# Float32 scores of both heads placed side by side, and weight preparation placed later, in a fused attention and FFN kernel

## The chip, the cores and the metric

The kernel runs on one core of one Trainium2 chip. The metric is the time of one execution in microseconds (us) on the device; less is better. The kernel before has a median of 722.2 us over three runs (721.16 to 723.02).

## What is computed

Attention with 4 batches, 8 heads, 768 positions and head size 64, float32. A query sees the keys at most `window` (128) positions back, and besides the first `n_sink` (4) positions. Its output, laid out as 3072 tokens by 512 features, goes through an FFN with 2048 hidden features and a gate.

```python
scores = scale * np.matmul(q, k.transpose(0, 1, 3, 2))
scores = np.where(is_sink | in_window, scores, -1000000000.0)
a = np.exp(scores - np.max(scores, axis=-1, keepdims=True))
a = a / (np.sum(a, axis=-1, keepdims=True) + 1e-09)
x = np.matmul(a, v)                  # to (3072, 512)
h = x @ w_in                         # (512, 2048)
g = h * np.clip(h + 3.0, 0.0, 6.0) / 6.0
out = g @ w_out                      # (2048, 512)
```

## The kernel before, in words

**Attention.** A unit is 256 query positions of one batch; there are 12 units, the four first units of the batches ahead of the others (L211, L212). A slot (`s`) is one pair of heads of one unit, so four slots make a unit and there are 48. One head of the pair lies on partitions 0 to 63 of the tiles `kr` and `qr`, the other on 64 to 127. The first ten slots are `plain` (L226): their scores are float32 matmuls over 64 partitions (L310), each of which the trace shows as two records, and two query tiles `t` per head make four scores in a slot, one of 128 and one of 256 columns per head. Later slots split K and Q into a high and a low part, move these parts together by DMA and use all 128 partitions (L315).

The steps of a slot, by the letters of the order list: `l` loads K and Q, `v` loads V, `k` and `q` split them (nothing in a plain slot), `c.s.h.t` is one score: a matmul, then on VectorE the masked minimum out of PSUM (L317); with the second tile of a head also the soft part (C_soft): exponentials on ScalarE (L339), sum and reciprocal on VectorE (L341, L342), and the norm (`norm`, L325 on ScalarE or L327 on VectorE by the letters of NORM0 while `s < START`, which is 9, and of NORM after). `d` transposes the probabilities (L365) and copies them out, `s` does the sink columns of later slots, `e` multiplies by V (L432); after the second head E_out makes xh and xl, a high and a low part (xl at L448 in plain slots). The tiles xh{p} and xl{p} have two buffers each.

**FFN.** When the fourth slot of a unit is done, its FFN is put into a queue as 34 steps (ffn_steps): for each of 8 weight slices two steps of ffn1 (12 matmuls of 256 columns each, L473), then, two slices later (one for the first two units), two steps of ffn2 (6 matmuls of 512 columns, L499), and two that write out. `f` in the order list drains one step. A step has the number of weight parts that it needs, and drain (L533) takes it only when that many have been loaded; if the first unit's next step isn't due, the second unit's may go.

**Weights.** There are 16 weight parts, w_in and w_out of a slice in turn. `w` loads the next one (load_part, L141): a DMA into a stage tile `st` of 64-bit words, two ScalarE activations (L159, L163) and two VectorE operations (L165, L167) that make a float32 tile `wt` out of them, a copy that rounds to the high part (L169, recorded at L35 on ScalarE; the letters of WHI give its engine), and a subtraction on VectorE that gives the low part (L170). `st` has three buffers, under the tags sb0, sb1 and K, `wt` has two, under w0 and kt; kt and K are those of the later slots' K too. `w.n` queues the part's work on VectorE and ScalarE behind slot n's last minimum and last exponential.

**Order.** The list FIRST (L554) gives the order of the steps of the first slots; from slot 16 on the loop at L613 goes through ORDER. The order of the list sets the priority; the framework's scheduler arranges each engine's instructions by it and by what is ready in its own estimate. `i.n` is keep_busy: n matmuls of 128 columns whose result nobody reads. There are 54 of them in FIRST and 10 ahead of it (L88), and each is two records of L86.

Of the kernel before, what the change touches and what calls it, by code (L numbers as in the profile page):

```python
# [9 lines left out]
F32 = mybir.dt.float32  # L10
# [4 lines left out]
ALU = mybir.AluOpType  # L15
# [29 lines left out]
def attn_ffn_kernel(ctx: ExitStack, tc: tile.TileContext, qx, kx, vx, vfx, vsx, n_sink, window, w_in, w_out, out):  # L45
    nc = tc.nc
    B, NU, NP = qx.shape[0:3]
    NT, DM = out.shape
    NFP = w_in.shape[0]
    H, D, UT = 2 * NP, 64, 256  # L50
# [78 lines left out]
    WOH = [const.tile([P, 2, DM], F32R, name=f"woh{i}") for i in range(NFP)]  # L129
    WOL = [const.tile([P, 2, DM], F32R, name=f"wol{i}") for i in range(NFP)]  # L130
    wide = mybir.dt.size(w_in.dtype) == 8
    WHI, WLO = "A", "D"

    def weng(which, at):
        return {"D": nc.vector, "P": nc.gpsimd, "A": nc.scalar}[which[at % len(which)]]
# [5 lines left out]
    def load_part(hi, lo, src, rows, at):  # L141

        def like(t):
            return t.rearrange("p (a b) -> p a b", a=rows)

        st = work.tile([P, PW, 2], I32, tag=("sb0", "sb1", "K")[at % 3 if at < LAST else at % 2], name="st", bufs=1)
        if not wide:
            st = like(st.rearrange("p n w -> p (n w)").bitcast(F32)[:, 0:PW])
            nc.sync.dma_start(out=st, in_=src)
            split_parts(nc, hi, lo, st, nc.scalar, nc.vector)  # L150
            return

# [8 lines left out]
        nc.scalar.activation(out=low, in_=low.bitcast(U32), func=AF.Copy, scale=2.0 ** -29 * (1 - 2.0 ** -18),  # L163
                             bias=7.5 * 2.0 ** -18 - 0.5)
        nc.vector.scalar_tensor_tensor(out=low, in0=high, scalar=-2 ** 31, in1=low,  # L165
                                       op0=ALU.bitwise_and, op1=ALU.bitwise_or)
        nc.vector.scalar_tensor_tensor(out=it, in0=it, scalar=3, in1=low,  # L167
                                       op0=ALU.logical_shift_left, op1=ALU.bitwise_or)
        copy_r(nc, weng(WHI, at), hi, like(ft))  # L169
        weng(WLO, at).tensor_tensor(out=lo, in0=like(ft), in1=hi.bitcast(F32), op=ALU.subtract)  # L170

    def load_w_in(i):
        load_part(WIH[i], WIL[i], w_in[i], NP, 2 * i)
# [359 lines left out]
    def drain(n):  # L533

        for _ in range(n):
            live = [q for q in queues if q]
            if not live:
                return
            if live[0] is queues[0] and len(live) > 1:
                order = live[0:2]  # L540
            else:
                order = live[0:1]
            for q in order:
                if q[0][0] <= 2 * NFP - len(w_order):
# [7 lines left out]

    FROM = 16
    FIRST = """  # L554
        l.0 l.1 k.0 q.0 v.0 v.1 c.0.0.0 k.1 c.0.0.1 c.0.1.0 c.0.1.1
        i.16 l.2 d.0.0 d.0.1 s.0 q.1 v.2 c.1.0.0 c.1.0.1 i.2 i.4 c.1.1.0 c.1.1.1
        e.0.0 k.2 l.3 e.0.1 q.2 i.6 d.1.0 s.1 w.0 m d.1.1 v.3 c.2.0.0 c.2.0.1 i.4 e.1.0 c.2.1.0 c.2.1.1
        l.4 i.2 k.3 d.2.0 q.3 v.4 d.2.1 c.3.0.0 e.1.1 l.5 c.3.0.1 s.2 i.2 c.3.1.0 c.3.1.1
        e.2.0 k.4 e.2.1 d.3.0 q.4 w i.12 d.3.1 s.3 v.5 e.3.0 c.4.0.0 w.2 c.4.0.1 k.5 c.4.1.0 c.4.1.1
        e.3.1 f s.4 q.5 l.6 w.2 f d.4.0 f v.6 w.3 c.5.0.0 f c.5.0.1 d.4.1 c.5.1.0 f k.6 f v.7 q.6 e.4.0 c.5.1.1  # L560
        l.7 e.4.1 f d.5.0 f.3 d.5.1 f.2 c.6.0.0 s.5 c.6.0.1 w f.2 c.6.1.0 e.5.0 f w.4 c.6.1.1
        k.7 e.5.1 q.7 l.8 w.5 f.2 d.6.0 f c.7.0.0 f d.6.1 f.3 v.8 f.2 s.6 f.2 c.7.0.1 e.6.0 c.7.1.0 c.7.1.1
        l.9 f.2 w e.6.1 k.8 q.8 i.2 f.2 s.7 w.5 w.7 f d.7.0 d.7.1 c.8.0.0 i.4 f c.8.0.1 c.8.1.0 f c.8.1.1
        f v.9 e.7.0 k.9 l.10 e.7.1 f q.9 w.8 f.2 w.6 f.2 d.8.0 c.9.0.0 f w.8 d.8.1 c.9.0.1 v.10 c.9.1.0 c.9.1.1
        s.8 l.11 e.8.0 k.10 f.2 q.10 f e.8.1 w.7 f s.9 d.9.0 d.9.1 c.10.0.0 f w.8 f.2 v.11 f.2 c.10.0.1 f.2 c.10.1.0 l.12 c.10.1.1
        e.9.0 f k.11 e.9.1 f q.11 d.10.0 s.10 f.4 v.12 f.2 c.11.0.0 c.11.0.1 d.10.1 f c.11.1.0 f.2 e.10.0 e.10.1 c.11.1.1
        d.11.0 f k.12 f.2 d.11.1 q.12 v.13 f l.13 c.12.0.0 f k.13 c.12.0.1 c.12.1.0 c.12.1.1
        f.3 s.11 q.13 e.11.0 f l.14 e.11.1 f.2 d.12.0 d.12.1 v.14 f s.12 c.13.0.0 f c.13.0.1 f c.13.1.0 l.15 k.14 c.13.1.1
        e.12.0 f k.15 e.12.1 q.14 d.13.0 f s.13 f c.14.0.0 f d.13.1 f v.15 f e.13.0 c.14.0.1 f c.14.1.0 f c.14.1.1
        e.13.1 q.15 d.14.0 s.14 f l.16 f.2 d.14.1 f.2  # L570
    """

    def slot_E(s, h):
# [14 lines left out]
    def do(step):  # L588
# [203 lines left out]
```

## Time and profile before

| | before |
|---|---|
| median of 3 runs | 722.2 us (721.16 to 723.02) |
| the profiled execution | 722.0 us |
| its span in the trace | 720.2 us |
| TensorE matmul busy | 706.3 us (98%) |
| VectorE busy | 495.9 us (69%) |
| ScalarE busy | 418.4 us (58%) |
| GpSimd busy | 173.7 us (24%) |
| mean granted TensorE clock | 0.998 |

The span goes from the first to the last instruction of the program; the 1.8 us between it and the execution's time lie around it. In the trace PE is TensorE's matmul, PEld its weight load, DVE is VectorE, ACT is ScalarE, POOL is GpSimd, and SPq is the queue on which SyncE issues DMAs. A group names the line, the engine, the operation, output<-inputs by the program's tile names, and the shapes. Matmuls are pipelined and their ends are modelled, so they overlap in the records, and busy time of TensorE includes its fillers. The chain of waits is followed back from the last instruction: each piece is what released the next one, or the instruction ahead of it on its engine.

### The profile page before, as it was taken

To read this page: it belongs to the slowest core of one execution; us is meant where nothing else is said; L and a number is where in the kernel's file an instruction comes from. 1 tells how busy PE (TensorE), PEld (TensorE's weight loads), DVE (VectorE), ACT (ScalarE), POOL (GpSimd) and SP (SyncE) were. 2 spreads that over 40 slices of the span, in tenths; PEclk is the share of its full clock that TensorE was granted. 3 is DMA by queue.
4 is the path that set the end of the run, shared out by engine and by line. 5 is a ranking of instruction groups with operands and counts; after the bars stand their busy time and mean duration, and the time that the engine had idled before them with its cause. 6 is when DMAs were issued, how large, how long until landed. Compare 5 with 4: busy or idle time off the path is not lost.

```text
span 720.2 us, 14250 instructions
## 1 busy us (share of the span) xinstructions
PE 706.3 (98%) x4800; PEld 639.1 (89%) x4800; DVE 495.9 (69%) x1365; ACT 418.4 (58%) x1091; POOL 173.7 (24%) x336
## 2 busy tenths in 40 slices
PE   8999999999999999999999999999999999999996
PEld 7777788989989988998999998998999999998995
DVE  4899996667777676776777777677776776543331
ACT  6998985646656655656656566655655665411211
POOL 1000000000035334334335334334333434200000
PEclk9999999999999999999999999999999999999999
DMA  8756745334544544554554554553553642000000
GB/s 292 247 191 206 261 128 161 84 97 129 128 126 139 138 115 121 144 141 121 141 128 134 136 125 106 153 128 97 140 149 101 154 119 71 31 1 1 30 1 34
DMA packets 53296, 89.10 MB, mean 124 GB/s; under 512 B 8160, under 2 KB 38112, under 8 KB 51168
## 3 DMA queue, kind: packets, MB, share of 16 engines
q1 hardware_dynamic: 53072, 88.11, 44.0%
q8 instruction: 40, 0.66, 0.4%
q14 instruction: 40, 0.33, 0.2%
q10 hardware_dynamic: 144, 0.00, 0.0%
HBM read 42.47 MB, written 6.29 MB: 68 GB/s over the span
## 4 chain that ended last, share of the span: by engine, by line
PE 88%; DMA 4%; ACT 3%; DVE 2%; SPq 2%; issue 1%; POOL 0%; ACTq 0%; DVEq 0%
PE hps L473 35%; PE o L499 35%; PE av L432 7%; PE sp L315 5%; PE pt L365 3%; DMA K<-kt 3%; PE sp L310 2%; SPq L265 1%; DMA st<-in_w_in_dram 1%; PE idle L86 1%; DMA raw<-in_n_sink_dram 1%; ACT Pt L339 0%; ACT Ph L339 0%; DVE kt L30 0%; DVE wt L167 0%
## 5 line engine op out<-in xcount | busy, mean ns | idle before, releaser
L473 PE MATMUL hps<-xh,wih 128*128 128x256 f32 x768 | 220.0, 286 | 1.3 <-ACT wih L35 1.1
L473 PE MATMUL hps<-xl,wih 128*128 128x256 f32 x768 | 216.2, 281 | 1.3 <-DVE xl L448 1.3
L473 PE MATMUL hps<-xh,wil 128*128 128x256 f32 x768 | 217.1, 283 | 0.0
L499 PE MATMUL o<-woh,gh 128*128 128x512 f32 x384 | 155.0, 404 | 0.0
L499 PE MATMUL o<-wol,gh 128*128 128x512 f32 x384 | 151.6, 395 | 0.0
L499 PE MATMUL o<-woh,g 128*128 128x512 f32 x384 | 151.3, 395 | 0.0
L473 PEld LDWEIGHTS hps<-xh,wih 128*128 128x128 f32 x768 | 144.7, 188 | 3.9 <-ACT wih L35 2.2
L473 PEld LDWEIGHTS hps<-xl,wih 128*128 128x128 f32 x768 | 144.9, 189 | 2.6 <-DVE xl L448 1.5
L473 PEld LDWEIGHTS hps<-xh,wil 128*128 128x128 f32 x768 | 144.7, 188 | 0.1
L486 DVE SCALAR_TENSOR_TENSOR gf<-gf,hps 128x512 f32<-128x512 f32 x96 | 65.8, 686 | 86.7 <-ACT gf L485 86.1
L347 POOL TENSOR_TENSOR Pt<-Pt 128x256 f32<-128x256 f32 x64 | 47.7, 745 | 295.9 <-ACT Pt L339 295.8
L485 ACT ACTIVATE gf<-hps,three 128x512 f32<-128x512 f32 x96 | 65.8, 685 | 84.9 <-PE hps L473 83.9
L339 ACT ACTIVATE Pt<-Pt,nb 128x272 f32<-128x272 f32 (+2 forms) x152 | 76.8, 506 | 63.0 <-DVE nb L317 62.5
L325 ACT ACTIVATE Pt<-Pt,rc 128x144 f32<-128x144 f32 (+2 forms) x152 | 55.8, 414 | 61.6 <-DVE rc L342 37.9
L499 PEld LDWEIGHTS o<-woh,g 128*128 128x128 f32 x384 | 72.2, 188 | 16.8
L499 PEld LDWEIGHTS o<-wol,gh 128*128 128x128 f32 x384 | 72.5, 189 | 10.4 <-DVE wol L170 0.3
L499 PEld LDWEIGHTS o<-woh,gh 128*128 128x128 f32 x384 | 72.4, 189 | 10.4 <-ACT woh L35 0.2
L488 DVE TENSOR_TENSOR g<-gf,gh 128x512 fp32r<-128x512 f32 x96 | 70.7, 736 | 0.8
L317 DVE CUSTOM_DVE_ANT_0 Pt<-sp,m_t 128x272 f32<-128x272 f32 x128 | 54.4, 430 | 17.5 <-PE sp L315 16.0
L315 PE MATMUL sp<-K 128*128 128x272 f32 (+2 forms) x304 | 60.5, 287 | 2.5 <-DMA K<-kt 2.5
L383 POOL TENSOR_SCALAR_AFFINE_SELECT ph<-ph 128x256 fp32r<-128x256 f32 x64 | 31.0, 485 | 118.6 <-ACT ph L35 118.6
L315 PEld LDWEIGHTS sp<-K 128*128 128x128 f32 x304 | 50.5, 188 | 9.5 <-DMA K<-kt 2.3
(93 smaller groups left out, 1089.8 us busy)
## 6 DMA issues: line engine op xcount, KB each, us to landing
K<-kt SPq DMA_DIRECT2D x128, 200.0 KB, 3.5
K<-kt SPq DMA_DIRECT2D x152, 64.0 KB, 2.4
st<-in_w_in_dram SPq DMA_DIRECT2D x8, 1024.0 KB, 5.3
st<-in_w_out_dram SPq DMA_DIRECT2D x8, 1024.0 KB, 5.2
kr<-in_kx_dram SPq DMA_DIRECT2D x32, 200.0 KB, 2.4
qr<-in_qx_dram SPq DMA_DIRECT2D x48, 128.0 KB, 2.3
out_dram<-ost SPq DMA_DIRECT2D x24, 256.0 KB, 2.6
vr<-in_vx_dram SPq DMA_DIRECT2D x32, 192.0 KB, 2.6
```

The costliest lines, as they stand in the source:

```text
L315: nc.tensor.matmul(out=sp[:, 0:w], lhsT=Q[:, h, t * P:(t + 1) * P], rhs=K[:, h, part, k0c:k0c + w], start=(part == 0), stop=(part == 1))
L317: d["min"] = nc.vector.tensor_tensor_reduce(out=cell(s, h, t, 0, w), in0=sp[:, 0:w], in1=m[:, 0:w], scale=-SCALE, scalar=3.0e38, op0=ALU.a ...
L325: nc.scalar.mul(out=blk, in_=blk, mul=c)
L339: d["exp"] = nc.scalar.activation(out=blk, in_=blk, func=AF.Exp, scale=-1.0, bias=nb[:, i:i + 1], accum_out=sm[:, i:i + 1])
L347: nc.gpsimd.tensor_tensor(out=both, in0=both, in1=prior, op=ALU.add)
L383: nc.gpsimd.affine_select(out=prior[i], in_=own[i], pattern=[[0, 2], [-1, P]], base=0, channel_multiplier=1, compare_op=ALU.is_gt, fill=0.0)
L432: nc.tensor.matmul(out=o, lhsT=l, rhs=r, start=(j == 0 and (h == 0 or not plain(s))), stop=(j == len(seq) - 1 and (h == 1 or not plain(s))))
L473: nc.tensor.matmul(out=hp[:, half, :], lhsT=l, rhs=r, start=(j == 0), stop=(j == n - 1))
L485: nc.scalar.activation(out=gf, in_=hp, func=AF.Relu, bias=three, scale=1.0)
L486: nc.vector.scalar_tensor_tensor(out=gf, in0=gf, scalar=6.0, in1=hp, op0=ALU.min, op1=ALU.mult)
L488: eng(GLO, state["n"] * NP).tensor_tensor(out=g, in0=gf, in1=gh.bitcast(F32), op=ALU.subtract)
L499: nc.tensor.matmul(out=acc, lhsT=l[:, f, ts_], rhs=r[i][:, f, :], start=(i == 0 and f == 0 and j == 0), stop=(i == NFP - 1 and f == 1 and ...
```

## The change

The four scores of a slot are issued in the order head 0, head 1 of one tile, then of the other, instead of both tiles of head 0 and then of head 1, and in most slots with fewer steps in between. The subtraction that makes the low half of a weight part is no longer done with the load: it is put into a list, and the new step `z` does the oldest one; drain counts a part as loaded only when its low half has been issued. The first load moves from the beginning of slot 2 to its end, and the last ones reach into slot 11. WHI gives the high copy of parts 0 and 12 to VectorE, NORM0 gives the norm of head 0's second tile (256 columns) to VectorE while `s < 9`. FIRST is a new list, with 72 matmuls of keep_busy instead of 54.

```diff
@@ -129,7 +129,7 @@
     WOH = [const.tile([P, 2, DM], F32R, name=f"woh{i}") for i in range(NFP)]
     WOL = [const.tile([P, 2, DM], F32R, name=f"wol{i}") for i in range(NFP)]
     wide = mybir.dt.size(w_in.dtype) == 8
-    WHI, WLO = "A", "D"
+    WHI, WLO = "DAAAAAAAAAAADAAA", "D"
 
     def weng(which, at):
         return {"D": nc.vector, "P": nc.gpsimd, "A": nc.scalar}[which[at % len(which)]]
@@ -167,7 +167,13 @@
         nc.vector.scalar_tensor_tensor(out=it, in0=it, scalar=3, in1=low,
                                        op0=ALU.logical_shift_left, op1=ALU.bitwise_or)
         copy_r(nc, weng(WHI, at), hi, like(ft))
-        weng(WLO, at).tensor_tensor(out=lo, in0=like(ft), in1=hi.bitcast(F32), op=ALU.subtract)
+        low_parts.append((lo, like(ft), hi))
+
+    low_parts = []
+
+    def low_part():
+        lo, whole, hi = low_parts.pop(0)
+        nc.vector.tensor_tensor(out=lo, in0=whole, in1=hi.bitcast(F32), op=ALU.subtract)
 
     def load_w_in(i):
         load_part(WIH[i], WIL[i], w_in[i], NP, 2 * i)
@@ -318,7 +324,7 @@
                                        scalar=3.0e38, op0=ALU.add, op1=ALU.min,
                                        accum_out=d["nb"][:, i:i + 1])
 
-    NORM0, NORM = "DADA", "AAAA"
+    NORM0, NORM = "DDDA", "AAAA"
 
     def norm(e, blk, c):
         if e == "A":
@@ -541,7 +547,7 @@
             else:
                 order = live[0:1]
             for q in order:
-                if q[0][0] <= 2 * NFP - len(w_order):
+                if q[0][0] <= 2 * NFP - len(w_order) - len(low_parts):
                     q.pop(0)[1]()
                     break
 
@@ -552,22 +558,22 @@
 
     FROM = 16
     FIRST = """
-        l.0 l.1 k.0 q.0 v.0 v.1 c.0.0.0 k.1 c.0.0.1 c.0.1.0 c.0.1.1
-        i.16 l.2 d.0.0 d.0.1 s.0 q.1 v.2 c.1.0.0 c.1.0.1 i.2 i.4 c.1.1.0 c.1.1.1
-        e.0.0 k.2 l.3 e.0.1 q.2 i.6 d.1.0 s.1 w.0 m d.1.1 v.3 c.2.0.0 c.2.0.1 i.4 e.1.0 c.2.1.0 c.2.1.1
-        l.4 i.2 k.3 d.2.0 q.3 v.4 d.2.1 c.3.0.0 e.1.1 l.5 c.3.0.1 s.2 i.2 c.3.1.0 c.3.1.1
-        e.2.0 k.4 e.2.1 d.3.0 q.4 w i.12 d.3.1 s.3 v.5 e.3.0 c.4.0.0 w.2 c.4.0.1 k.5 c.4.1.0 c.4.1.1
-        e.3.1 f s.4 q.5 l.6 w.2 f d.4.0 f v.6 w.3 c.5.0.0 f c.5.0.1 d.4.1 c.5.1.0 f k.6 f v.7 q.6 e.4.0 c.5.1.1
-        l.7 e.4.1 f d.5.0 f.3 d.5.1 f.2 c.6.0.0 s.5 c.6.0.1 w f.2 c.6.1.0 e.5.0 f w.4 c.6.1.1
-        k.7 e.5.1 q.7 l.8 w.5 f.2 d.6.0 f c.7.0.0 f d.6.1 f.3 v.8 f.2 s.6 f.2 c.7.0.1 e.6.0 c.7.1.0 c.7.1.1
-        l.9 f.2 w e.6.1 k.8 q.8 i.2 f.2 s.7 w.5 w.7 f d.7.0 d.7.1 c.8.0.0 i.4 f c.8.0.1 c.8.1.0 f c.8.1.1
-        f v.9 e.7.0 k.9 l.10 e.7.1 f q.9 w.8 f.2 w.6 f.2 d.8.0 c.9.0.0 f w.8 d.8.1 c.9.0.1 v.10 c.9.1.0 c.9.1.1
-        s.8 l.11 e.8.0 k.10 f.2 q.10 f e.8.1 w.7 f s.9 d.9.0 d.9.1 c.10.0.0 f w.8 f.2 v.11 f.2 c.10.0.1 f.2 c.10.1.0 l.12 c.10.1.1
-        e.9.0 f k.11 e.9.1 f q.11 d.10.0 s.10 f.4 v.12 f.2 c.11.0.0 c.11.0.1 d.10.1 f c.11.1.0 f.2 e.10.0 e.10.1 c.11.1.1
-        d.11.0 f k.12 f.2 d.11.1 q.12 v.13 f l.13 c.12.0.0 f k.13 c.12.0.1 c.12.1.0 c.12.1.1
-        f.3 s.11 q.13 e.11.0 f l.14 e.11.1 f.2 d.12.0 d.12.1 v.14 f s.12 c.13.0.0 f c.13.0.1 f c.13.1.0 l.15 k.14 c.13.1.1
-        e.12.0 f k.15 e.12.1 q.14 d.13.0 f s.13 f c.14.0.0 f d.13.1 f v.15 f e.13.0 c.14.0.1 f c.14.1.0 f c.14.1.1
-        e.13.1 q.15 d.14.0 s.14 f l.16 f.2 d.14.1 f.2
+        l.0 l.1 k.0 q.0 k.1 v.0 v.1
+        c.0.0.0 q.1 c.0.1.0 c.0.0.1 c.0.1.1 i.12 l.2 d.0.0 d.0.1 s.0 k.2
+        c.1.0.0 c.1.1.0 c.1.0.1 c.1.1.1 e.0.0 i.4 v.2 i.2 s.1 e.0.1 l.3 d.1.0 d.1.1 q.2 v.3
+        c.2.0.0 c.2.1.0 i.4 c.2.0.1 c.2.1.1 e.1.0 l.4 s.2 e.1.1 i.4 k.3 q.3 m i.12 d.2.0 w.0 v.4 d.2.1
+        c.3.0.0 c.3.1.0 w.1 l.5 c.3.1.1 z c.3.0.1 e.2.0 z i.4 k.4 w.2 i.8 z q.4 i.2 d.3.0 e.2.1 w.3 s.3 d.3.1 i.6 l.6
+        c.4.0.0 z v.5 e.3.0 c.4.1.0 c.4.0.1 k.5 c.4.1.1 i.8 e.3.1 w.2 z f w.2 f i.4 d.4.0 q.5 d.4.1 f s.4 f i.2 z
+        c.5.0.0 c.5.1.0 c.5.0.1 v.6 c.5.1.1 w.4 f.2 e.4.0 f w.4 f e.4.1 v.7 k.6 l.7 z q.6 w.4 f.2 z d.5.0 d.5.1
+        c.6.0.0 c.6.0.1 s.5 z c.6.1.0 c.6.1.1 f.2 e.5.0 e.5.1 k.7 q.7 w f w l.8 f z z d.6.0 s.6 k.8 f.4
+        c.7.0.0 v.8 c.7.1.0 d.6.1 c.7.0.1 q.8 c.7.1.1 e.6.0 e.6.1 f l.9 f.2 w f z
+        c.8.0.0 d.7.0 f.2 d.7.1 f c.8.0.1 f.3 v.9 f.3 c.8.1.0 c.8.1.1 f.5 s.7 k.9 f e.7.0 e.7.1 f q.9 l.10 f.2 d.8.0 d.8.1 v.10 w.7 s.8
+        c.9.0.0 c.9.1.0 z e.8.0 f c.9.0.1 f l.11 c.9.1.1 s.9 f e.8.1 f k.10 f q.10 d.9.0 f d.9.1 w.8
+        c.10.0.0 f v.11 k.11 f c.10.0.1 f q.11 f c.10.1.0 z e.9.0 e.9.1 w.9 c.10.1.1 l.12 f s.10 z d.10.0 f.2 d.10.1 f v.12
+        c.11.0.0 f c.11.1.0 c.11.1.1 f c.11.0.1 f e.10.0 k.12 w.10 s.11 l.13 f.2 e.10.1 q.12 d.11.0 k.13 f d.11.1 f
+        c.12.0.0 f c.12.1.0 c.12.0.1 c.12.1.1 e.11.0 f.3 e.11.1 z f.2 v.13 d.12.0 l.14 d.12.1 f q.13 f
+        c.13.0.0 c.13.1.0 s.12 c.13.1.1 c.13.0.1 k.14 f.3 v.14 q.14 e.12.0 s.13 e.12.1 f l.15 v.15 f d.13.0
+        c.14.0.0 c.14.1.0 c.14.0.1 d.13.1 c.14.1.1 f e.13.0 k.15 f l.16 f.3 d.14.0 s.14 d.14.1 e.13.1 q.15 f
     """
 
     def slot_E(s, h):
@@ -592,6 +598,8 @@
             drain(n[0] if n else 1)
         elif kind == "w":
             weights(n[0] if n else None)
+        elif kind == "z":
+            low_part()
         elif kind == "i":
             keep_busy(n[0])
         elif kind == "m":
```

## Rows read from the trace of the kernel before

**Rows 1.** Busy time of each engine by stretch; after PEclk the DMA share, GB/s

```profile
core 0: us, PE busy (x) PEld busy (x) DVE busy (x) ACT busy (x) POOL busy (x), PEclk, DMA share, GB/s
6.70:35.00 28.30, 27.11 (x185) 22.35 (x184) 21.54 (x76) 26.16 (x65) 0.63 (x3) 1.00 0.82 300
35.00:60.00 25.00, 23.59 (x144) 19.48 (x143) 24.10 (x54) 23.23 (x46) 0.00 (x0) 1.00 0.62 216
60.00:90.00 30.00, 28.85 (x180) 24.14 (x179) 27.44 (x62) 26.36 (x49) 0.00 (x0) 1.00 0.67 222
90.00:110.00 20.00, 19.98 (x134) 17.43 (x133) 19.09 (x37) 17.37 (x33) 0.00 (x0) 1.00 0.46 134
...
600.00:700.00 100.00, 100.00 (x666) 91.19 (x665) 42.16 (x99) 24.38 (x55) 9.24 (x20) 1.00 0.08 22
```

**Rows 2.** Chain of waits in order of time, 0 to 130 us: start, us, what

```profile
10.24 1.02 issue
...
12.13 0.59 ACT st L163
...
14.41 0.76 ACT wt L159
...
22.25 1.12 DVE wt L167
...
35.33 1.14 DVE st L165
...
36.61 1.12 DVE wt L167
...
38.25 1.93 PE hps L473 x14
...
50.59 1.43 PE hps L473 x12
...
70.43 0.98 ACT Ph L339 x4
...
72.73 1.07 ACT wih L35
...
78.72 0.69 ACT gf L485
79.41 0.95 ACT wih L35
```

**Rows 3.** Timeline of ScalarE: start, us, then the instruction; idle before it in brackets

```profile
10.21 1.14 ACT L159 ACTIVATE wt<-st 128x1024 f32<-128x1024 f32 x1 [0.91 <-DMA st<-in_w_in_dram]
```

**Rows 4.** Timeline of TensorE, neighbours of one line merged

```profile
5.84 0.93 PE L310 MATMUL sp<-kr,qr 64*128 64x128 f32 x8 [0.53 <-DMA qr<-in_qx_dram]
6.71 3.84 PE L86 MATMUL idle<-rel 128*128 128x128 f32 x32
...
18.02 0.92 PE L310 MATMUL sp<-kr,qr 64*128 64x128 f32 x4
...
56.80 0.92 PE L310 MATMUL sp<-kr,qr 64*128 64x128 f32 x6
```

**Rows 5.** Busy time by stretch of L310 alone: PE, PEld, clock, DMA

```profile
10.00:32.50 22.50, 5.52 (x24) 3.11 (x24) 1.00 0.78 275
32.50:100.00 67.50, 10.79 (x48) 5.63 (x48) 1.00 0.59 200
```

**Rows 6.** ScalarE groups, 35.1 to 110.1 us: count, busy us, mean ns, idle before

```profile
L35 ACT ACTIVATE wih<-wt 128x1024 fp32r<-128x1024 f32 x6 | 6.3, 1058 | 0.0
...
L325 ACT ACTIVATE Ph<-Ph,rc 128x256 f32<-128x256 f32 x12 | 5.9, 501 | 0.0
```

**Rows 7.** VectorE groups of the same stretch

```profile
L317 DVE CUSTOM_DVE_ANT_0 Ph<-sp,m 128x256 f32<-128x256 f32 x11 | 4.6, 417 | 0.8 <-PE sp L310 0.8
L41 DVE CAST gh<-gf 128x512 fp32r<-128x512 f32 x8 | 3.4, 420 | 0.0
L317 DVE CUSTOM_DVE_ANT_0 Ph<-sp,m 128x128 f32<-128x128 f32 x10 | 2.9, 285 | 0.4 <-PE sp L310 0.4
L327 DVE TENSOR_SCALAR Ph<-Ph,rc 128x128 f32<-128x128 f32 x10 | 2.7, 279 | 0.0
```

## Prediction

> **What bounds the kernel now.** I read the stretches first, then the chain of waits in order of time, then single groups. In the stretches [rows 1] the reader is to see two halves. From 600 us on TensorE is busy 100.00 of 100 us while VectorE needs 42.16 and ScalarE 24.38: nothing but matmul is left, so whatever time TensorE wastes earlier is still missing at the end, and whatever it saves earlier comes off the end. Until 110 us all three engines are close to full: ScalarE 26.16 of 28.30 us before 35, VectorE 24.10 of 25, 27.44 of 30 and 19.09 of 20 after that. The change acts there; the loop from slot 16 on is not touched.
>
> A busy TensorE is not a useful one, since fillers count as busy, so the chain decides [rows 2]. Up to 38.25 us it is mixed: pieces on ScalarE and VectorE that belong to weight parts (L159, L163, L165, L167) stand between attention steps. At 10.24 the norm of slot 0's second head waits 1.02 us because ScalarE first does weight part 0's L159, for which it sat idle 0.91 us until the transfer landed [rows 3]. The five pieces 12.13, 14.41, 22.25, 35.33 and 36.61 add 0.59 + 0.76 + 1.12 + 1.14 + 1.12 = 4.73 us, so 5.75 us of the chain up to the first unbroken run of FFN matmuls are weight work. From 38.25 to 110 the chain is nearly all TensorE; the two breaks of over a microsecond are those that end with the weight copies at 72.73 and 79.41 (3.4 us from 70.43, 1.6 us from 78.72). So a TensorE instruction saved there counts, as long as VectorE, with 0.90 + 2.56 + 0.91 = 4.4 us free in 75, follows.
>
> **The change, part by part.**
>
> *Scores side by side.* In slot 0 of the kernel before, nothing stands between the four scores on TensorE, and the eight records (float32 makes two of each matmul) take 0.93 us; from slot 1 on the two heads are apart and one head alone takes 0.92 [rows 4]. At 56.80 six records of both heads take 0.92 too. So the two heads, on partitions 0 to 63 and 64 to 127, already run at the same time when they are neighbours, at no cost to either. By stretches [rows 5] slots 1 to 3 take 5.52 us and slots 4 to 9 take 10.79. At 0.93 a slot that would be 2.79 and 5.58: 2.7 us saved before the FFN, 5.2 us in it. The first 2.7 us I cost at nothing: fillers stand in the same stretch (16 in the 3.84 us after slot 0), so TensorE waits there. Of the 5.2, the new order keeps slots 4 to 7 together but for single steps; in slot 8 transposes and FFN steps stand between all the pairs, and in slot 9 between the second ones. I leave these two out, a third of six slots, and take 3.4. Ends: 0 (the engine that reads the scores sets the pace) and 5.2.
>
> *Weights later.* w.0 moves from slot 2's beginning to its end, behind d.2.0, and the loads come in ones and twos until slot 11 (before: slot 10). Each load still issues one transfer on SyncE, two activations and a copy on ScalarE and three operations on VectorE. The transfer moves later with it, past v.3 and l.4 on SyncE's queue, which gives these two their turn earlier, and ScalarE no longer sits waiting for it at 10 us. Parts 0 to 3 still come ahead of the first FFN step, so their work cannot leave the stretch, only move out of attention's way. ScalarE is the fullest there. It loses one 256-wide norm in each of four slots and part 0's copy [rows 6]: with 0.50 and 1.06 us, and about 0.1 of each covered by its neighbour, 4 x 0.4 + 1.0 = 2.6 us. I take 2.6 us off the start of the FFN. Ends: 0 (the weights are merely missed later) and 5.75 (all of it leaves the chain).
>
> *Norms and two copies on VectorE.* The 256-wide norm there is bounded by the 128-wide one, 0.28, and by twice that; the reading of a 256-wide score, 0.42, is nearest [rows 7], 0.34 behind a neighbour. Part 0's and part 12's copy, 1024 wide, lie between one and three times the 512-wide cast at 0.42; I take 0.75, as twice the columns with one start. Slots 4 to 8 and part 12 fall into the stretch where VectorE is 91 to 96% busy: 5 x 0.34 + 0.75 = 2.5 us. Slots 0 to 3 and part 0, 2.1 us, fall where it has 6.8 us free [rows 1] and cost nothing; without that cover they would be 2.1 more. Of the 2.5 I count 1.5, since the chain there runs on TensorE and 4.4 us are free. Ends: 0 and 4.6 for both stretches.
>
> *Low halves as steps.* The same subtraction, 16 times as before, placed by hand. The buffer that it reads stays taken until then, so the second load after it (and k.11, which shares one with part 13) waits for it; behind k.11 on ScalarE queue slot 11's activations and its scores. By then unit 1's FFN steps are there to run; cost nothing, at most one subtraction where they are not.
>
> *Fillers.* There are 54 matmuls of keep_busy before and 72 after, all 18 new ones ahead of the FFN. At 3.84/16 = 0.24 us [rows 4] they are 4.3 us of TensorE, which the 2.7 us of scores saved there and TensorE's waiting, which the fillers of before already fill, cover; where TensorE is what holds the start up, +1.6.
>
> *New order.* Counted through the lists, 22 FFN steps are issued ahead of slot 8's scores where it was 14, but 63 by the end of the list where it was 71. A step is 12 small matmuls, 1.43 us [rows 2], so about 11 us of FFN move behind the list and none disappears. They end in the last stretch, where TensorE is full anyway: cost nothing. Attention that runs further ahead has to wait for the two xh buffers; what it waits for is FFN, so TensorE is not idle.
>
> **Sum.** -2.6 (start) - 3.4 (scores) + 1.5 (VectorE) = -4.5 us on the profiled execution's 722.0, which is 0.2 below the median of the runs. That gives 717.5.
>
> **Rivals.**
>
> *VectorE reads the scores no faster.* A slot's four scores cost it 2 x (0.29 + 0.42) = 1.4 us [rows 7] by durations, over the 0.93 that TensorE then needs. If each pair waits for that, the 3.4 us turn into waits: -2.6 + 1.5, 720.9. Against it: between two slots TensorE has FFN steps, so the pace of one slot need not show. The Trainium skill, TensorEngine Tiling (Array Packing), Performance Considerations, says the same as a rule: tiling speeds up the matmul engine but not the emptying of PSUM, which may become the bottleneck. By that rule the scores would bring nothing, and the trace agrees so far as 1.4 exceeds 0.93. Chance 0.2, most of it within the band of no change.
>
> *VectorE becomes the bound (slower).* The place is 35 to 110 us. If neither its 6.8 free us before 35 nor its 4.4 after are used, every added operation shows, 2.1 + 2.5 = 4.6 us, and neither start nor scores help, since TensorE then waits for g and for low halves: 722.0 + 4.6 = 726.6; with the 2.1 still covered, 724.5. It decides from the point where added work exceeds free time in the FFN's stretch: 2.5 against 4.4 speaks against it, 95% busy for it. Chance 0.15.
>
> *The start falls away.* All 5.75 us leave the chain, the breaks at 70 and 78 us go (5.0) because unit 1 is there earlier, and scores bring 3.4: with half of the breaks, 722.0 - 5.75 - 2.5 - 3.4 + 1.5 = 711.9. For it: the chain shows exactly those pieces. Against it: the weights have to be made sometime, on engines that are full. Chance 0.2.
>
> *The order doesn't do what it says.* The trace shows instructions on ScalarE in another order than the list has them (part 0's first activation ahead of slot 0's last norm, though w.0 stands after slot 1 there), so the placing need not survive, and slots 4 and 6 were partly together already. Then -1 to -2: 720.5. It shares the chance of the first rival.
>
> **How the numbers follow.** Forecast 0.45, about 715 to 719.8; quick start 0.2; no gain 0.2; VectorE 0.15. About 0.3%, 2.2 us, is what a measurement of this kernel can tell from no change. So faster 0.65, same 0.2, slower 0.15. The range goes from 711, just past the quick start, to 724.5, which leaves out the worst of the VectorE case: some 2 in 10 stay outside. The forecast's own range is 715 to 720.
>
> **What would show it.** Scores: L310 in slots 4 to 7 as groups of eight records of about 0.93, and under 8 us of L310 from 32 to 100 us. Start: no wait of a norm behind L159 at 10 us, and the unbroken run of FFN matmuls from 35 to 36 us (38.25 before). VectorE: over 97% busy from 35 to 110 if the slower rival is right, with hps and o waiting for g, wil or wol. The last weight part is done later than before, without a wait of o. The prediction is wrong if the FFN starts no earlier, or if TensorE's gaps in 38 to 110 grow by what L310 loses.

## The result and the profile after

The changed kernel takes 715.32 us (median of 4 runs, 715.13 to 716.19) against 722.28 us of the kernel before on the same chip (4 runs, 721.16 to 723.02). The ratio is 0.9907, with a 95% interval from 0.989 to 0.9924: 7.0 us, or 0.9%, faster. The forecast was 717.5 us in a range from 711 to 724.5; the sign was right, the gain 2.5 us too small, and the time stands at the low end of the forecast's own 715 to 720. A second sample of the changed kernel, shown below, gave 0.9913. One execution of the run with the pairs alone took 1144.77 us at a mean clock of 0.556, and no ratio uses it.

In the changed kernel the lines after the edit stand six further down: the scores' L310 is L316, the norms' L325 and L327 are L331 and L333, the FFN's L473 and L499 are L479 and L505, and the subtraction for the low half is L176. The profiled execution took 716.19 us, the slowest of the four.

The head of the profile page: span, then busy time of each engine.

```profile
span 714.5 us, 14315 instructions
...
PE 703.5 (98%) x4836; PEld 640.3 (90%) x4836; DVE 496.0 (69%) x1376; ACT 413.3 (58%) x1080; POOL 173.2 (24%) x336
```

The same stretches as in [rows 1], with the loop from 200 to 600 us added:

```profile
core 0: us, PE busy (x) PEld busy (x) DVE busy (x) ACT busy (x) POOL busy (x), PEclk, DMA share, GB/s
6.70:35.00 28.30, 27.66 (x209) 23.51 (x207) 24.98 (x83) 26.05 (x60) 0.74 (x4) 1.00 0.81 304
35.00:60.00 25.00, 23.48 (x173) 21.25 (x173) 23.63 (x49) 21.77 (x41) 0.00 (x0) 1.00 0.71 253
60.00:90.00 30.00, 30.00 (x200) 25.89 (x200) 29.32 (x75) 26.10 (x55) 0.00 (x0) 1.00 0.53 169
90.00:110.00 20.00, 20.00 (x129) 17.79 (x130) 18.05 (x47) 15.96 (x39) 0.00 (x0) 1.00 0.58 187
...
200.00:600.00 400.00, 399.24 (x2802) 367.35 (x2802) 292.56 (x849) 242.24 (x689) 156.25 (x293) 1.00 0.48 126
600.00:700.00 100.00, 100.00 (x654) 90.97 (x653) 36.59 (x67) 17.38 (x31) 3.68 (x8) 1.00 0.03 11
```

Three things are to be seen. Before 35 us VectorE took over work (24.98 us where it was 21.54), yet ScalarE is as busy as before, 26.05 against 26.16: what it was relieved of was filled up again, by weight parts (the two activations of a part, L159 and L163, take 11.5 us there where they took 9.2). From 35 to 110 us ScalarE needs 63.8 us where it needed 67.0, and VectorE, with 71.0 of 75 us, is no fuller than before (70.6). And TensorE has no gap from 60 to 90 us, where it had 1.15 us.

The scores' line alone, the counterpart of [rows 5] (busy time of TensorE, then of its weight loads, clock, DMA):

```profile
10.00:32.50 22.50, 3.86 (x25) 2.06 (x26) 1.00 0.79 287
32.50:100.00 67.50, 6.94 (x48) 3.77 (x48) 1.00 0.63 213
```

48 records that took 10.79 us take 6.94. The timeline of TensorE (start, duration, instruction, idle time before it in brackets) has the start of the FFN and a pair of heads in one group. First the FFN's first matmul in the kernel before, then the changed kernel:

```profile
35.13 0.37 PE L473 MATMUL hps<-xh,wih 128*128 128x256 f32 x1
```

```profile
36.95 0.36 PE L479 MATMUL hps<-xh,wih 128*128 128x256 f32 x1
...
38.22 0.83 PE L86 MATMUL idle<-rel 128*128 128x128 f32 x6
38.81 0.37 PE L479 MATMUL hps<-xl,wih 128*128 128x256 f32 x1
...
44.81 0.93 PE L316 MATMUL sp<-kr,qr 64*128 64x128 f32 x8
47.26 0.47 PE L505 MATMUL o<-woh,gh 128*128 128x512 f32 x1 [1.52 <-DVE gh L41]
```

Eight records of both heads take 0.93 us at 44.81, what one head alone took at 18.02 in [rows 4]. The first FFN matmul comes at 36.95 us, 1.8 us later than before, and the run without fillers between its matmuls starts at 38.81, against 38.25 in [rows 2]. So the FFN does not start earlier. (Second traces of the two kernels, from the last experiment below, have 35.26 and 36.95.)

Of the profiled spans' 5.7 us (720.2 to 714.5), busy sums explain part: TensorE's gaps between 6.7 and 700 us shrink from 6.3 to 3.7 us (2.6 us), the scores after 10 us from 16.3 to 10.8 (5.5 us), and fillers after 6.7 us grow from 14.16 to 18.01 (-3.85 us). That is 4.3 us; the other 1.4 such sums cannot place, since neighbouring matmuls overlap in them.

### The profile page after: what moved, and what is told of

Its sections match the earlier page's. It is cut to its first block, busy times and chain, and to the rows that moved or that the text cites. A ratio compares the mean times of both kernels' runs of the same rounds, so it can differ in the third digit from the quotient of the medians.

```text
span 714.5 us, 14315 instructions
## 1 busy us (share of the span) xinstructions
PE 703.5 (98%) x4836; PEld 640.3 (90%) x4836; DVE 496.0 (69%) x1376; ACT 413.3 (58%) x1080; POOL 173.2 (24%) x336
## 5 line engine op out<-in xcount | busy, mean ns | idle before, releaser
L479 PE MATMUL hps<-xh,wih 128*128 128x256 f32 x768 | 219.2, 286 | 0.3 <-DVE tmp L460 0.3
L479 PE MATMUL hps<-xh,wil 128*128 128x256 f32 x768 | 216.6, 282 | 0.0
L479 PE MATMUL hps<-xl,wih 128*128 128x256 f32 x768 | 215.9, 281 | 0.0
L505 PE MATMUL o<-woh,gh 128*128 128x512 f32 x384 | 154.2, 402 | 1.5 <-DVE gh L41 1.5
L505 PE MATMUL o<-woh,g 128*128 128x512 f32 x384 | 151.4, 395 | 0.0
L505 PE MATMUL o<-wol,gh 128*128 128x512 f32 x384 | 151.3, 394 | 0.0
L479 PEld LDWEIGHTS hps<-xh,wih 128*128 128x128 f32 x768 | 144.6, 188 | 2.0 <-PE sp L321 0.5
L479 PEld LDWEIGHTS hps<-xl,wih 128*128 128x128 f32 x768 | 144.8, 188 | 1.2
L479 PEld LDWEIGHTS hps<-xh,wil 128*128 128x128 f32 x768 | 144.6, 188 | 0.1
L331 ACT ACTIVATE Pt<-Pt,rc 128x144 f32<-128x144 f32 (+2 forms) x152 | 55.3, 414 | 60.4 <-DVE rc L348 36.4
L505 PEld LDWEIGHTS o<-woh,g 128*128 128x128 f32 x384 | 72.2, 188 | 17.3 <-issue 0.3
L505 PEld LDWEIGHTS o<-woh,gh 128*128 128x128 f32 x384 | 72.3, 188 | 11.8 <-ACT gf L491 1.9
L505 PEld LDWEIGHTS o<-wol,gh 128*128 128x128 f32 x384 | 72.4, 189 | 10.3
```

The lines of the kernel that those rows point to most:

```text
L331: nc.scalar.mul(out=blk, in_=blk, mul=c)
L479: nc.tensor.matmul(out=hp[:, half, :], lhsT=l, rhs=r, start=(j == 0), stop=(j == n - 1))
L505: nc.tensor.matmul(out=acc, lhsT=l[:, f, ts_], rhs=r[i][:, f, :], start=(i == 0 and f == 0 and j == 0), stop=(i == NFP - 1 and f == 1 and ...
```

## The experiments

Each ratio is to the kernel before on the same chip, from 5 to 12 executions; 0.0014 of it is 1 us. The theory after the result: paired scores shorten TensorE's path, and the rest comes from fewer waits in the new order. The rival: the scores were covered anyway, and the work moved between ScalarE and VectorE made the gain.

**Pairs alone.** In the order of before, the four scores of each of slots 0 to 9 are put together where the first stood; nothing else is changed.

```diff
-        i.16 l.2 d.0.0 d.0.1 s.0 q.1 v.2 c.1.0.0 c.1.0.1 i.2 i.4 c.1.1.0 c.1.1.1
+        i.16 l.2 d.0.0 d.0.1 s.0 q.1 v.2 c.1.0.0 c.1.1.0 c.1.0.1 c.1.1.1 i.2 i.4
...
-        k.7 e.5.1 q.7 l.8 w.5 f.2 d.6.0 f c.7.0.0 f d.6.1 f.3 v.8 f.2 s.6 f.2 c.7.0.1 e.6.0 c.7.1.0 c.7.1.1
+        k.7 e.5.1 q.7 l.8 w.5 f.2 d.6.0 f c.7.0.0 c.7.1.0 c.7.0.1 c.7.1.1 f d.6.1 f.3 v.8 f.2 s.6 f.2 e.6.0
```

> The kernel before with one edit in its order list: the four scores of each plain slot stand together at the place of the first. Theory (paired scores are TensorE time saved in the FFN's stretch): the busy time of L310 in slots 4 to 9 falls from 10.79 to about 6 us and the time falls by 3 to 4 us, to about 718.5. Rival (the pairing shows only in the order that the weights have in the changed kernel, since VectorE reads the scores no faster): L310 falls as much and the time stays within 1.5 us of 722.3.

Measured: 721.16 us, ratio 0.9988 (0.9975 to 1.0002). That looks like the rival, but the stretches (columns as above) say otherwise:

```profile
20.00:25.00 5.00, 2.57 (x16) 2.08 (x14) 4.83 (x14) 5.00 (x13) 0.00 (x0) 0.89 0.77 243
25.00:30.00 5.00, 5.00 (x18) 3.16 (x18) 3.63 (x11) 4.02 (x11) 0.00 (x0) 0.50 0.51 200
30.00:35.00 5.00, 3.44 (x23) 2.92 (x22) 3.34 (x10) 4.01 (x9) 0.00 (x0) 0.93 0.92 289
```

and TensorE's timeline just there:

```profile
24.02 0.66 PE L365 MATMUL pt<-ident_r,Ph 128*128 128x128 f32 x2 [2.43 <-DVE Ph L327]
...
27.29 1.23 PE L310 MATMUL sp<-kr,qr 64*128 64x256 f32 x4
```

With the scores shorter, TensorE was done early and waited 2.43 us for a norm; the granted clock fell to 0.50, the 1.2 GHz level, and came back to 1.00 only between 30 and 35 us. Read from the three means, it was low for 1.1 + 5.0 + 0.7 = 6.8 us. The kernel before holds 1.00 in that stretch [rows 1]. Its compared executions list a mean clock of 0.990 to 0.996 over the span, those of the kernel before beside them 0.997 to 1.0. The Trainium skill, TensorE: Matmul & The Clock Gate, section on HAM oscillation, says that waits between groups of matmuls can put the engine back to the slow clock; this trace agrees (a wait of 2.43 us, then 0.50).

**Pairs and sixteen fillers.** The same with fillers put where TensorE waits.

```diff
-        l.4 i.2 k.3 d.2.0 q.3 v.4 d.2.1 c.3.0.0 c.3.1.0 c.3.0.1 c.3.1.1 e.1.1 l.5 s.2 i.2
-        e.2.0 k.4 e.2.1 d.3.0 q.4 w i.12 d.3.1 s.3 v.5 e.3.0 c.4.0.0 c.4.1.0 c.4.0.1 c.4.1.1 w.2 k.5
+        l.4 i.2 k.3 i.10 d.2.0 q.3 v.4 d.2.1 c.3.0.0 c.3.1.0 c.3.0.1 c.3.1.1 e.1.1 l.5 s.2 i.2
+        e.2.0 k.4 e.2.1 i.6 d.3.0 q.4 w i.12 d.3.1 s.3 v.5 e.3.0 c.4.0.0 c.4.1.0 c.4.0.1 c.4.1.1 w.2 k.5
```

> The paired scores in the order of the kernel before (as in e1_pairs_alone), with 16 more matmuls of keep_busy where TensorE waited there, ahead of d.2.0 and d.3.0. Theory (in e1_pairs_alone the pairing's gain was given back because the granted clock fell to 0.5 for 6.8 us after a wait of 2.4 us that score matmuls used to fill): the clock stays at 1.00 from 7 us on and the time falls by 2 to 4 us against e1_pairs_alone's ratio of 0.9988, to about 718.5. Rival (the score time saved was not on the path in that order): the clock stays up and the time stays within 1.5 us of 721.

Measured: 717.07 us, ratio 0.9946 (0.9933 to 0.996): 3.9 us faster than before and 3.0 us faster than the pairs alone. The first stretch, then the scores' line:

```profile
6.70:35.00 28.30, 26.42 (x206) 22.93 (x204) 22.48 (x71) 27.04 (x63) 0.73 (x4) 1.00 0.85 305
```

```profile
32.50:105.00 72.50, 6.25 (x48) 3.43 (x48) 1.00 0.62 209
```

The clock holds 1.00, and the scores, 10.79 us before in this stretch too, take 6.25: 4.5 us of TensorE less, for a gain of 3.9 in the old order, on the old engines and with low halves made at once. The two numbers can't simply be set against each other, though, as the loop of the profiled execution (716.13 us, the fastest of its six) shows:

```profile
200.00:600.00 400.00, 400.00 (x2819) 368.86 (x2818) 296.04 (x853) 245.56 (x696) 160.38 (x296) 1.00 0.50 129
```

TensorE has no gap there. In the kernel before it has 2.5 and 2.0 us in two traces (shown further down), so 2.0 to 2.5 us of this execution's gain lie in a part that no edit touches. From 35 to 110 us, on the other hand, its gaps are 3.5 us where they were 2.6, and the first FFN matmul comes at 36.66 us, 1.5 later than before. How much of the 3.9 us reaches the time through the shorter scores alone is therefore not shown, and the sixteen fillers were not tried without the pairs.

**The change without eighteen fillers.** They are taken out of slot 3's row.

```diff
-        c.3.0.0 c.3.1.0 w.1 l.5 c.3.1.1 z c.3.0.1 e.2.0 z i.4 k.4 w.2 i.8 z q.4 i.2 d.3.0 e.2.1 w.3 s.3 d.3.1 i.6 l.6
+        c.3.0.0 c.3.1.0 w.1 l.5 c.3.1.1 z c.3.0.1 e.2.0 z k.4 w.2 z q.4 i.2 d.3.0 e.2.1 w.3 s.3 d.3.1 l.6
```

> The changed kernel without 18 of its matmuls of keep_busy (those of slot 3's row: 4, 8 and 6), so with 54 as before. Theory (the new fillers hold the clock up while TensorE waits): a stretch at 0.5 appears between 20 and 45 us and the time rises by 1.5 to 4 us above 715.3. Rival (they are TensorE time on the way to the first FFN step): the clock stays at 1.00, the first FFN matmul comes 1 to 4 us earlier than at 36.95 and the time falls by 1 to 4 us.

Measured: 722.02 us, ratio 1.001 (0.9996 to 1.0023): the whole gain is gone. Stretches, and the largest wait of TensorE in the first 130 us (us in total, times, longest):

```profile
25.00:30.00 5.00, 2.10 (x14) 1.73 (x12) 5.00 (x17) 4.90 (x12) 0.00 (x0) 0.92 0.74 283
30.00:35.00 5.00, 4.51 (x17) 3.59 (x18) 4.22 (x8) 4.71 (x8) 0.00 (x0) 0.50 0.61 211
35.00:40.00 5.00, 5.00 (x26) 4.30 (x22) 3.63 (x11) 2.45 (x9) 0.00 (x0) 0.56 0.39 100
```

```profile
PE pt L371 <- DVE Ph L333: 4.3, 2, 3.4
```

With a wait of 3.4 us the clock falls, and it is low for 0.8 + 5.0 + 4.4 = 10.2 us, into the FFN. So matmuls that compute nothing are worth 7 us here, more than the theory's 1.5 to 4. At half speed 10.2 us are at most 5.1 us of work, so the clock can be the larger part of it but not all: TensorE also has gaps of 0.9 us from 60 to 90 us, where the changed kernel has none, and of 1.9 in the loop, where it has 0.8. Why these came is not shown.

**Heads apart again.** In the changed kernel the second head's scores of slots 1 to 9 are set at least one TensorE step behind the first's.

```diff
-        c.5.0.0 c.5.1.0 c.5.0.1 v.6 c.5.1.1 w.4 f.2 e.4.0 f w.4 f e.4.1 v.7 k.6 l.7 z q.6 w.4 f.2 z d.5.0 d.5.1
+        c.5.0.0 c.5.0.1 v.6 w.4 f.2 c.5.1.0 c.5.1.1 e.4.0 f w.4 f e.4.1 v.7 k.6 l.7 z q.6 w.4 f.2 z d.5.0 d.5.1
...
-        c.7.0.0 v.8 c.7.1.0 d.6.1 c.7.0.1 q.8 c.7.1.1 e.6.0 e.6.1 f l.9 f.2 w f z
+        c.7.0.0 c.7.0.1 v.8 d.6.1 c.7.1.0 c.7.1.1 q.8 e.6.0 e.6.1 f l.9 f.2 w f z
```

> The changed kernel with the two heads' scores of slots 1 to 9 set apart by one other TensorE step. Theory (pairing is worth its TensorE time): L316 in slots 4 to 9 rises from 6.94 to about 10.5 us and the time rises by 3 to 4 us above the changed kernel's 715.3, to about 719. Rival (the gain is that of the weights' order and of the backlog): within 1.5 us of 715.3.

Measured: 724.14 us, ratio 1.003 (1.0017 to 1.0043), 9 us slower than the change, more than the theory's 3 to 4. The scores' line:

```profile
32.50:105.00 72.50, 11.03 (x48) 6.21 (x48) 1.00 0.60 202
```

It takes 11.03 us again, 4.1 more than in the changed kernel. The loss is more than that: in the profiled execution (722.72 us, at a mean clock of 0.998) the line also takes 5.52 us from 10 to 32.5 us (3.86 in the changed kernel), TensorE waits 2.5 us for VectorE's norms in the first 130 us (0.4 there), and the first FFN matmul comes at 41.10 us (36.95 there). The slowest executions (725.1 to 727.0) list a mean clock of 0.993 to 0.995. The order was made for scores that come together.

**Low halves made at once.** In the changed kernel the subtraction goes back behind the load, and the steps z fall out.

```diff
         copy_r(nc, weng(WHI, at), hi, like(ft))
-        low_parts.append((lo, like(ft), hi))
+        weng(WLO, at).tensor_tensor(out=lo, in0=like(ft), in1=hi.bitcast(F32), op=ALU.subtract)
...
-        c.4.0.0 z v.5 e.3.0 c.4.1.0 c.4.0.1 k.5 c.4.1.1 i.8 e.3.1 w.2 z f w.2 f i.4 d.4.0 q.5 d.4.1 f s.4 f i.2 z
+        c.4.0.0 v.5 e.3.0 c.4.1.0 c.4.0.1 k.5 c.4.1.1 i.8 e.3.1 w.2 f w.2 f i.4 d.4.0 q.5 d.4.1 f s.4 f i.2
```

> The changed kernel with each low half made with its load, as in the kernel before, and z doing nothing. Theory (low halves as steps of their own cost and bring nothing, since the scheduler places them by priority anyway): within 1.5 us of 715.3. Rival (a low half ahead of scores on VectorE's queue delays attention in the first slots): 2 to 4 us above it, with VectorE's reads of scores waiting behind L170.

Measured: 719.23 us, ratio 0.9954 (0.9941 to 0.9967): 3.4 us slower than the change by the ratios. TensorE's largest waits in the first 130 us:

```profile
PE o L505 <- ACT st L163: 2.1, 1, 2.1
PE pt L371 <- ACT Ph L331: 1.7, 1, 1.7
```

In the changed kernel TensorE waits 1.5 us for gh at the first L505 instead, and 0.3 us for L331. The clock falls to its low level behind each of them, as the stretches from 6.7 to 35 us (mean 0.94) and from 35 to 60 us (0.93) list, but that profile is of the slowest execution (722.82 us, mean clock 0.992 over the span). The two at 0.998 and above took 718.30 and 718.29, so some 3 us are lost without the clock.

**The old engines.** Norms and copies go back to the engines of before.

```diff
-    WHI, WLO = "DAAAAAAAAAAADAAA", "D"
+    WHI, WLO = "A", "D"
...
-    NORM0, NORM = "DDDA", "AAAA"
+    NORM0, NORM = "DADA", "AAAA"
```

> The changed kernel with the norms of head 0's second tile and the copies of weight parts 0 and 12 back on ScalarE. Theory (ScalarE is the fuller engine up to the first FFN step, VectorE after it): the first FFN matmul comes 1 to 2.6 us later than at 36.95, VectorE has 4 us less in 0 to 110, and the time is about 1 us above 715.3. Rival (VectorE is the bound in the FFN's stretch): 1.5 to 4 us below 715.3.

Measured: 717.51 us, ratio 0.9927 (0.9914 to 0.994), 1.0 to 1.4 us slower than the two samples of the change, whose intervals it overlaps. What the theory asked for is in the trace: the first FFN matmul comes 1.0 us later, and VectorE is busy 94.07 us up to 110 us where it is 97.53 in the changed kernel.

```profile
37.93 0.36 PE L479 MATMUL hps<-xh,wih 128*128 128x256 f32 x1
```

So VectorE's new work does no harm, and in this order ScalarE's relief is worth about 1 us at the start of the FFN.

**The new engines in the old order.** The same two constants of the change, put into the kernel with pairs and sixteen fillers.

```diff
-    WHI, WLO = "A", "D"
+    WHI, WLO = "DAAAAAAAAAAADAAA", "D"
...
-    NORM0, NORM = "DADA", "AAAA"
+    NORM0, NORM = "DDDA", "AAAA"
```

> The order of the kernel before with paired scores and 16 more fillers (as in e5_pairs_fillers, ratio 0.9946), and the changed kernel's norms and weight copies on VectorE. Theory (ScalarE is the fuller engine ahead of the FFN, as e4_engines showed in the new order with 0.9927 against 0.9907): 1 to 2 us below e5_pairs_fillers, a ratio near 0.9925. Rival (the moves pay only with the new order's placing of weights): within 0.7 us of 0.9946, or above it.

Measured: 718.18 us, ratio 0.9947 (0.9934 to 0.996), against 0.9946 without them: nothing. In this order the FFN starts no sooner for it (37.60 us against 36.66).

**Late low halves in the old order.** The changed kernel's code with the order of the last run, and each z put six places behind its w.

```diff
-        e.3.1 f s.4 q.5 l.6 w.2 f d.4.0 f v.6 w.3 c.5.0.0 c.5.1.0 c.5.0.1 c.5.1.1 f d.4.1 f k.6 f v.7 q.6 e.4.0
+        e.3.1 f s.4 q.5 l.6 z w.2 f d.4.0 f v.6 w.3 c.5.0.0 z c.5.1.0 c.5.0.1 c.5.1.1 f d.4.1 z f k.6 f v.7 q.6 e.4.0
```

> The code of the changed kernel with the order of e5_pairs_fillers, and each low half as a step six places behind its load. Theory (pairs with fillers, engine moves and late low halves are the whole gain, and the rest of the new order is worth nothing): a ratio of 0.990 to 0.992, like the changed kernel. Rival (the new order as a whole is needed to use late low halves): no better than e11_pairs_engines.

Measured: 724.9 us, ratio 1.0045 (1.0029 to 1.0061), slower than the kernel before. A stretch, and TensorE's largest waits until 130 us:

```profile
90.00:110.00 20.00, 16.92 (x120) 15.37 (x118) 18.89 (x33) 16.07 (x32) 0.00 (x0) 1.00 0.48 140
```

```profile
PE pt L371 <- DVE Ph L333: 2.0, 4, 1.2
PE sp L321 <- DMA K<-kt: 1.9, 1, 1.9
PE o L505 <- ACT gf L491: 1.2, 1, 1.2
```

Only the low halves differ from the run before, and with them when drain lets a step go, since a part counts only with its low half. They cost 7 us (1.0045 less 0.9947). Some of that is clock: three of the six executions list 0.993 or 0.994 and took 725.9 to 726.6 us, while the two at 0.998 took 722.2 and 723.0, 4 to 5 us more than the run before. In the new order it was 3 us dearer to make them at once. So neither place is good in itself; six places was one choice among many, and others weren't tried.

**The first load early.** In the changed kernel w.0 goes back to the beginning of slot 2.

```diff
-        c.2.0.0 c.2.1.0 i.4 c.2.0.1 c.2.1.1 e.1.0 l.4 s.2 e.1.1 i.4 k.3 q.3 m i.12 d.2.0 w.0 v.4 d.2.1
+        w.0 c.2.0.0 c.2.1.0 i.4 c.2.0.1 c.2.1.1 e.1.0 l.4 s.2 e.1.1 i.4 k.3 q.3 m i.12 d.2.0 v.4 d.2.1
```

> The changed kernel with the first weight load back at the beginning of slot 2, all else unchanged. Theory (the scheduler fits part 0 into ScalarE's gaps either way; its place in the list moves little): within 1.5 us of 715.3. Rival (part 0 in the way of slots 0 to 2 is what the kernel before paid at 10 us): 2 to 4 us above it.

Measured: 715.42 us, ratio 0.9916 (0.9902 to 0.9929), the same as the change. ScalarE's timeline shows why, first in the changed kernel and then in this one:

```profile
10.30 1.13 ACT L159 ACTIVATE wt<-st 128x1024 f32<-128x1024 f32 x1 [0.90 <-DMA st<-in_w_in_dram]
11.34 0.49 ACT L331 ACTIVATE Ph<-Ph,rc 128x256 f32<-128x256 f32 x1
```

```profile
10.33 1.14 ACT L159 ACTIVATE wt<-st 128x1024 f32<-128x1024 f32 x1 [1.11 <-DMA st<-in_w_in_dram]
11.37 0.50 ACT L331 ACTIVATE Ph<-Ph,rc 128x256 f32<-128x256 f32 x1
```

Either way ScalarE turns to part 0 at 10.3 us and sits idle for its transfer, as in [rows 3], and the norm stands behind it. Moving w.0 in the list did not move this work in the instruction stream.

**The change without six late fillers.** Those among the first FFN steps are taken out.

```diff
-        c.4.0.0 z v.5 e.3.0 c.4.1.0 c.4.0.1 k.5 c.4.1.1 i.8 e.3.1 w.2 z f w.2 f i.4 d.4.0 q.5 d.4.1 f s.4 f i.2 z
+        c.4.0.0 z v.5 e.3.0 c.4.1.0 c.4.0.1 k.5 c.4.1.1 i.8 e.3.1 w.2 z f w.2 f d.4.0 q.5 d.4.1 f s.4 f z
```

> The changed kernel without the six matmuls of keep_busy that stand among the first FFN steps. Theory (TensorE has work there, so they are on its path): about 1 us below 715.3, since six of them are 12 records at about 0.11 us. Rival (they fill waits): within 0.7 us of 715.3, with idle time in their place.

Measured: 718.83 us, ratio 0.9964 (0.9952 to 0.9976), 4 us slower than the change, with the clock at 1.00 in every stretch. Both theories missed this. Its largest wait in the first 130 us:

```profile
PE o L505 <- DVE gh L41: 2.1, 1, 2.1
```

It was 1.5 us in the changed kernel's first trace and 2.1 us in its second, shown next, so it does not explain the loss by itself. TensorE's gaps from 35 to 110 us are 3.0 us where they were 1.5 (2.1 in the second trace), and instructions far behind the six stand in another order. How much of the 4 us is that order and how much the wait stays open.

**Both kernels once more.** No edit: one more execution of the kernel before and five more of the changed one, to see what repeats.

> The kernel before once more, for a second trace. Theory (part of the gain is in the loop from slot 16 on: TensorE was busy 397.48 of 400 us there before, 399.24 after): again about 397.5 between 200 and 600 us. Rival (that difference is one of single executions): between 398.5 and 400.

> The changed kernel once more, on the same chip as the experiments beside it. Every theory: a ratio of 0.990 to 0.992, granted clock 1.00 from 7 us to the tail, and TensorE busy about 399 of 400 us between 200 and 600 us.

Measured: 721.67 us for the kernel before. The changed kernel took 715.9 us, ratio 0.9913 (0.99 to 0.9926). The loop, first in the two executions of the kernel before and then in the changed kernel's second one:

```profile
200.00:600.00 400.00, 397.48 (x2788) 365.62 (x2788) 295.06 (x843) 243.79 (x690) 159.94 (x299) 1.00 0.50 128
```

```profile
200.00:600.00 400.00, 398.04 (x2791) 366.08 (x2790) 294.88 (x844) 243.86 (x690) 161.94 (x299) 1.00 0.49 128
```

```profile
35.00:60.00 25.00, 22.89 (x156) 20.52 (x155) 22.52 (x48) 19.72 (x38) 0.00 (x0) 0.93 0.67 232
...
200.00:600.00 400.00, 399.21 (x2809) 367.70 (x2808) 293.47 (x851) 242.21 (x690) 157.51 (x296) 1.00 0.48 126
```

TensorE waits 1.2 to 1.8 us less in the loop after the change, although no line there is edited. (The second trace before, 398.04, lies between what the theory and the rival asked for.) The runs shown above have between none (pairs with fillers) and 1.9 us (without eighteen fillers), so what is done ahead of the loop moves its waits. They are mostly for K, before and after:

```profile
PE sp L315 <- DMA K<-kt: 2.5, 5, 1.0
```

```profile
PE sp L321 <- DMA K<-kt: 0.5, 2, 0.3
```

Why its transfers come in better time was not tried and stays open. The profiled execution of the changed kernel lost the clock once, with 0.93 in 35 to 60 us, about 3.5 us at the low level, after a wait for gh of 2.1 us that was 1.5 in the first profile; it took 717.46 us, the slowest of its five. So the fillers do not hold the clock every time.

No variant was faster than the changed kernel.

## Why the prediction was right, and where its terms were wrong

**Scores side by side: right about TensorE, its share of the time not shown.** The term was -3.4 us. The line loses 3.85 us in the stretch that the prediction named, 6.94 us is under the 8 us asked for, and the loss did not turn into waits: TensorE's gaps from 38 to 110 us are 1.5 us where they were 1.4. That TensorE's neighbours on different halves of the partitions run at the same time was read correctly from [rows 4]. Where the pairs stand was forecast less well: groups of eight records were to come in slots 4 to 7 and came in slots 5 and 6 alone (44.81 and 57.80 us), while slots 8 and 9, left out of the term, are partly paired too. In time, the pairs with fillers bring 3.9 us, but in the profiled execution 2.0 to 2.5 of its gain lie in the loop. The part before the FFN, costed at nothing, cannot be parted from this.

**VectorE reads no faster: the rival fell.** Reading four scores still takes VectorE 1.4 us in the changed kernel, longer than the 0.93 us of TensorE, but the time did not stay at the rival's 720.9. By the rule of the Trainium skill, TensorEngine Tiling (Array Packing), Performance Considerations, which speaks of a fourfold speedup, the emptying of PSUM may become the limit; no run here shows it.

**Start of the FFN: wrong.** The step that failed is "I take 2.6 us off the start of the FFN", and the prediction's own sign, wrong "if the FFN starts no earlier", came true: the first FFN matmul comes 1.8 us later, and the unbroken run begins at 38.81 us where 35 to 36 was forecast. Two things were missed. ScalarE's freed time went in part to the next weight part: before 35 us its norms fell from 4.1 to 2.0 us, the weight activations rose by 2.3, and it is as busy as before. With the old engines the new order starts at 37.93 us, so the relief is worth 1.0 of the 2.6 us. And something else in the change moves the start back: pairs with fillers alone, in the old order, already start at 36.66 us. What it is there that delays the start was not tried. Part of the reasoning also rested on w.0 leaving attention's way, and it did not: the norm at 10 us waits behind L159 as before. That is what the rival "The order doesn't do what it says" had foreseen, though not with its time, 720.5.

The gain came later and in another form. The fourth low half begins at 35.4 us where it began at 41.1, the ninth at 63.7 where it was 73.8, TensorE has no gap from 60 to 90 us, and by 110 us it has issued 240 of the first and 96 of the second FFN matmuls where it had 230 and 84. That the earlier weights closed the gap is likely but not shown: without six late fillers the ninth low half begins at 63.6 us too, and 0.9 us of gap stay. Of the quick start's price, the 5.75 us off the chain did not come; of the 5.0 us of breaks at 70 and 78 us no more was to be had than the 1.15 us for which TensorE had stood still there.

**Low halves cost nothing: wrong.** "Cost nothing, at most one subtraction" holds for the instruction and not for its place. In the new order the place is worth about 3 us; in the old one late low halves cost 7, or 4 to 5 in the executions that keep the clock. The prediction named the buffer behind them as the price but never asked what VectorE could do first.

**Norms and copies on VectorE: right in sum with ScalarE's relief.** The prices read from the rows held: a norm takes 0.345 us on VectorE and a copy 0.69, together 2.4 us in the FFN's stretch (2.5 forecast). Of these +1.5 us was taken as cost, apart from the 2.6 us of relief, whereas only the sum of both can be measured: -2.6 + 1.5 = -1.1, and undoing the move makes the new order 1.0 to 1.4 us slower. As far as the start tells (1.0 us), the relief was put too high and the cost too high by about as much, which is luck. VectorE stays at 71.0 of 75 us, so the slower rival lacked its condition, work above free time.

**Fillers: the right number for a wrong reason.** Nothing was counted for them because TensorE waits there. True, but they are not idle ballast: without 18 of them the change is worth nothing. The prediction spoke of no clock at all, because it is 1.00 in every stretch of [rows 1]. With the pairs alone it is not: they take work from TensorE just where it waits.

**The sum.** Pairs with fillers bring 3.9 us, and all that the change has beyond that 2.4 to 2.8 more, by the ratios of its two samples. This second part belongs to the order as a whole: early low halves cost it 3 us, the old engines 1, six fillers fewer 4, and together these are more than it has to give, so they are no separate terms. That 717.5 lies within 2.2 us of the time is in part luck: the earlier start did not come, the clock and the loop had no term, and the order as a whole, costed at nothing, made up for the start. (Of the counts in the prediction one is off, with no term resting on it: the old list issues 17 FFN steps ahead of slot 8's scores, not 14.) What remains unsettled is the loop's 1.2 to 1.8 us, and what in the order makes the second part.

## What to carry to other kernels

Where TensorE waits for other engines, ask what a shorter matmul does to its granted clock: the same pairing was worth nothing with the clock lost and 3.9 us with sixteen idle matmuls in the waits. Time that is freed on a full engine goes at least in part to whatever is next in its stream: of 2.6 us expected at the stage's start, 1.0 came. An order written by hand is worth what it is as a whole: its parts beyond the pairs, tried one by one in another order, brought nothing or cost 7 us, and whether a step moved at all must be read from the trace.

## What the runs showed of the hardware

Float32 scores of two heads on different halves of the partitions run at the same time when they are neighbours on TensorE: at 44.81 us eight records of both heads take 0.93 us, what four of one head take. In the changed kernel a slot whose pairs stand apart pays for it: slot 7, with transposes between its two pairs, takes 0.49 + 0.70 us. The granted clock fell to the 1.2 GHz level during or just behind single waits of 1.7 to 3.4 us between busy pieces, and stayed there for some 3.4 to 10.2 us; one wait of 1.5 us in the changed kernel passed without it, and one of 2.1 us in the run without six fillers did too. At the low clock four records of two heads' 256-wide scores took 1.23 us (27.29 us in the run with pairs alone), and 0.70 us at the full one (72.66 us in the changed kernel).
